# The first loads of a fused attention and MLP kernel in another order: two tiles of x, the q and k weights in two transfers, then the other two tiles

## The chip, the cores and the metric

The kernel runs on one core of one Trainium2 chip. The metric is device time in microseconds for one execution. A core has TensorE (PE, matmul), VectorE (DVE), ScalarE (ACT), GpSimd (POOL) and SyncE (SP, here an issuer of DMAs). Each runs its own instructions in order, and they wait for each other by semaphores. DMAs are issued by SP and ACT into a hardware queue each (q1 and q10 in the profile) and by GpSimd into a software queue.

## The reference

A pre-norm attention block with a dilated sliding window, then a pre-norm gated MLP (ReGLU), over 2048 rows of 512 in bf16:

```python
h  = x + A(layernorm(x))
h2 = h + B(layernorm(h))

def A(x):                         # 32 heads of 16, window of 8 keys, dilation 2
    q, k, v = split(x @ wqkv)     # wqkv: 512 x 1536
    logits[s, w] = q[s] . k[s - 2 w] * 16 ** -0.5      # w = 0..7, masked where s - 2 w < 0
    o[s] = sum_w softmax(logits[s])[w] * v[s - 2 w]
    return o @ wo                 # 512 x 512

def B(x):
    gate, up = x @ W_gate, x @ W_up                    # 512 x 1376 each
    return (relu(gate) * up) @ W_down                  # 1376 x 512
```

## The kernel before

The rows are worked in four chunks of 512 (`tk` = 0 to 3), each of four row tiles of 128 (`j` = 0 to 3). For a chunk the kernel normalises the rows, transposes them into `xnT`, projects to q, k and v, forms q*k products on VectorE, sums them per head with small matmuls, takes the softmax, multiplies by v on VectorE, applies `wo`, adds the residual, normalises again and runs the MLP. All steps of all chunks are put into one list by a planner (`Plan`): every step has an engine, a planned duration and dependencies, and a fixed table (`RANK`) gives each step its rank, so each engine's instructions stand in a fixed order. Load times enter the planner as constants (`xload`, `wload`), not from the DMA instructions themselves.

`setup()` runs ahead of the planned steps. It issues the first loads from SP and ACT alternately: `x_sm` tiles 0 to 3 (128 KB each, L291), `wqk_sb` in four transfers of 256 KB, one for each 128 rows of the q and k weights (L293), then from SP rows 512 to 1023 of x (512 KB, L294). GpSimd copies one element of tile 0 into `wv_sb` (L308) so that the load of the v weights (L309) goes out only after tile 0 has landed; the same trick at L310 holds the later chunks of x (L312) until rows 512 to 1023 have landed. Then come `wo`, the MLP weights, and constants built on GpSimd and VectorE. SP's later loads also wait for the completion of the transfer that used the same completion semaphore eight hardware DMAs earlier; in the profile that is L294, which waits for an x tile.

The first chunk's path, by line:

- L431 `bn_stats` and L434 `bn_aggr` on VectorE, for each row tile; L444 and L448 on ACT turn the variance into 1/std; L466 on VectorE normalises a tile into `row`.
- L495 transposes a tile on TensorE (four 128x128 matmuls), L511 (ACT, tiles 0 and 2) and L509 (VectorE, tiles 1 and 3) copy the transposed tile into `xnT` (`quad` in the profile).
- L385 is a run of 44 dummy matmuls on TensorE at the start, L393 eight more after the transposes of tile 0 and of tile 1.
- L536 is the projection. For the first four q and k outputs it is done in two halves: 256 columns (tiles 0 and 1), then the other 256 (tiles 2 and 3). On TensorE the order is: first halves of the first two outputs (8 matmuls), transposes of tiles 2 and 3, then 24 more half-width matmuls. The very first of them waits for all `wqk_sb` loads in turn and for the copy of tile 1.
- L544 copies the results out on ACT, and L583 forms the first q*k product on VectorE.

VectorE's order in the first chunk is: statistics of tiles 0 and 1, normalise tile 0, statistics of tile 3, normalise tile 1, statistics of tile 2, copy of transposed tile 1, normalise tiles 3 and 2, then statistics of the next chunk.

Of the kernel before, what the change touches and what calls it, by code (L numbers as in the profile page):

```python
# [190 lines left out]
def kernel(  # L191
# [11 lines left out]
    nc = tc.nc  # L203
    Bsz, S, D = A_x.shape
# [3 lines left out]
    NT = D // P  # L208
# [15 lines left out]
    BPC = CS // P  # L224
# [4 lines left out]
    x_rows = A_x.rearrange("b (tb p) d -> p (b tb) d", p=P)  # L229
# [20 lines left out]
    x_sm = sb.tile([P, NTB, D], BF16, name="x_sm")  # L250
    wqk_sb = sb.tile([P, NT, 2 * D], BF16, name="wqk_sb")
# [35 lines left out]
    def setup():  # L287

        w3_r = A_wqkv.rearrange("(dt p) f -> p dt f", p=P)
        for j in range(BPC):  # L290
            (nc.scalar if j % 2 else nc.sync).dma_start(x_sm[:, j:j + 1, :], x_rows[:, j:j + 1, :])  # L291
        for dt in range(NT):
            (nc.scalar if dt % 2 else nc.sync).dma_start(wqk_sb[:, dt:dt + 1, :], w3_r[:, dt:dt + 1, 0:2 * D])  # L293
        nc.sync.dma_start(x_sm[:, BPC:2 * BPC, :], x_rows[:, BPC:2 * BPC, :])  # L294
        nc.scalar.preload_act_table_set("natural_log_exp_and_others")
        V.memset(warm[:], 0.0)
        make_identity(nc, identity[:])
        nc.gpsimd.memset(eps_t[:], EPS)
        nc.gpsimd.iota(ci[:], pattern=[[0, 1]], base=0, channel_multiplier=1)
        nc.gpsimd.iota(sel_i[:], pattern=[[1, H]], base=0, channel_multiplier=0)  # L300
        nc.gpsimd.iota(sp_i[:], pattern=[[1, H], [0, DQ]], base=0, channel_multiplier=0)
        nc.gpsimd.iota(sm_i, pattern=[[0, 4], [1, H]], base=0, channel_multiplier=0)
        nc.gpsimd.iota(mk_i[:], pattern=[[1, PADL]], base=0, channel_multiplier=0)
        nc.gpsimd.memset(kT[:, :, 0:PADL], 0.0)
        nc.gpsimd.memset(vT[:, :, 0:PADL], 0.0)


        nc.gpsimd.tensor_copy(out=wv_sb[0:1, 0, 0:1], in_=x_sm[0:1, 0, 0:1])  # L308
        nc.sync.dma_start(wv_sb[:], w3_r[:, :, 2 * D:3 * D])  # L309
        nc.gpsimd.tensor_copy(out=x_sm[0:1, 2 * BPC, 0:1], in_=x_sm[0:1, BPC, 0:1])  # L310
        for tk in range(2, NCK):
            nc.sync.dma_start(x_sm[:, tk * BPC:(tk + 1) * BPC, :], x_rows[:, tk * BPC:(tk + 1) * BPC, :])  # L312

        nc.sync.dma_start(wo_sb[:], A_wo.rearrange("(p t) f -> p t f", t=NT))
        nc.sync.dma_start(wu_sb[:], B_W_up.rearrange("(dt p) f -> p dt f", p=P))
        nc.sync.dma_start(wg_sb[:], B_W_gate.rearrange("(dt p) f -> p dt f", p=P))
        nc.sync.dma_start(
            wd_sb[:, 0:NFF, :], B_W_down[0:NFF * P, :].rearrange("(ft p) n -> p ft n", p=P))
        if FTAIL:
            nc.sync.dma_start(wd_sb[:FTAIL, NFF, :], B_W_down[NFF * P:F, :])  # L320


        for n, (op, by) in enumerate(((ALU.arith_shift_right, 2), (ALU.bitwise_and, H - 1),
                                      (ALU.arith_shift_right, 5))):
            V.tensor_scalar(out=tmp[:, n:n + 1], in0=ci[:], scalar1=by, scalar2=None, op0=op)
        V.tensor_copy(out=cf[:, 0:3], in_=tmp[:])
        V.tensor_scalar(out=cf[:, 2:3], in0=cf[:, 2:3], scalar1=1.0 * DIL, scalar2=None, op0=ALU.mult)
        V.tensor_scalar(out=cf[:, 3:4], in0=cf[:, 2:3], scalar1=4.0 * DIL, scalar2=None, op0=ALU.add)
        V.tensor_scalar(out=sel[:], in0=sel_i[:], scalar1=cf[:, 0:1], scalar2=None, op0=ALU.is_equal)
        V.tensor_scalar(out=spread[:], in0=sp_i[:], scalar1=cf[:, 1:2], scalar2=None, op0=ALU.is_equal)  # L330
        V.tensor_scalar(out=same[:], in0=sm_i, scalar1=cf[:, 1:2], scalar2=None, op0=ALU.is_equal)
        for hf in range(2):
            V.tensor_scalar(out=mask[:, hf, :], in0=mk_i[:], scalar1=cf[:, 2 + hf:3 + hf],
                            scalar2=None, op0=ALU.is_ge)
# [540 lines left out]
    with tc.manual_schedule():  # L875
        setup()
        for op in todo:
            if op.fn is not None:
                op.fn()
# [35 lines left out]
```

## Time and profile before

| | before |
|---|---|
| runs, us | 201.94, 201.73, 202.31; median 201.94 |
| profiled execution, span from first to last instruction, us | 202.4 |
| TensorE busy | 194.1 us, 96% of the span |
| VectorE busy | 152.8 us, 75% |
| ACT busy | 111.1 us, 55% |
| granted TensorE clock, mean | 0.992 |
| x_sm loads of 128 KB, issue to landing | 2.8 us (SP) and 3.0 us (ACT), median |
| wqk_sb loads of 256 KB, issue to landing | 6.8 to 7.9 us, median 7.4 |
| x_sm rows 512 to 1023, issue to landing | 7.5 us |
| wv_sb load, issue to landing | 8.4 us |

The span runs from the first to the last instruction of one profiled execution; the profile states no other time for that execution, and the runs of the table are other executions. Times in the profile count from the span's start. An engine with a `q` behind its name is that engine's sequencer, which issues DMAs. "PEclk" is the granted TensorE clock, as a share of full speed. In a timeline a row gives start, length, engine, line, operation, what it writes and reads, how often, and in brackets how long the engine was idle before it and what ended that.

### The profile page before, as it was taken

The numbers are of one execution on the slowest core, as the hardware profiler recorded it, in microseconds if no ns is written. First come the engines' busy times: TensorE is split into PE (matmuls) and PEld (weight loads), VectorE is DVE, ScalarE is ACT, GpSimd is POOL, SyncE is SP. The second block draws the span as 40 slices with busy tenths as digits, with TensorE's granted clock in tenths as the row PEclk, the third lists the DMA queues.
The fourth block names the chain that finished last, engine by engine and source line by source line (L and its number), as shares of the span: only waits on it lengthen the run. The fifth ranks groups of instructions, "written<-read, shape, count | busy, mean of one in ns | idle before, by whom it ended". The sixth has DMA issues, their size and how long they took to land.

```text
span 202.4 us, 2934 instructions
## 1 busy us (share of the span) xinstructions
PE 194.1 (96%) x1072; PEld 97.0 (48%) x1091; DVE 152.8 (75%) x239; ACT 111.1 (55%) x232; POOL 12.7 (6%) x28
## 2 busy tenths in 40 slices
PE   8699999999999999998999999999999999999994
PEld 8585545555335444443444444444444444444542
DVE  6678999998999989998989768999966521142332
ACT  3337699766698855673641846802277821454700
POOL 3000000330000003300103100000000000000000
PEclk9969999999999999999999999999999999999999
DMA  5969980699000534996086883130200320002003
GB/s 147 322 201 328 409 265 19 135 189 177 3 0 0 130 80 78 191 181 172 3 156 129 163 211 100 26 79 0 78 29 0 74 56 0 0 3 78 0 0 130
DMA packets 21133, 21.97 MB, mean 109 GB/s; under 512 B 8736, under 2 KB 17920, under 8 KB 21120
## 3 DMA queue, kind: packets, MB, share of 16 engines
q1 hardware_dynamic: 18672, 14.65, 24.9%
q0 software_dynamic: 1728, 6.29, 16.9%
q10 hardware_dynamic: 720, 0.85, 1.2%
q8 instruction: 8, 0.13, 0.3%
q14 instruction: 5, 0.04, 0.1%
HBM read 8.42 MB, written 2.10 MB: 52 GB/s over the span
## 4 chain that ended last, share of the span: by engine, by line
PE 67%; DVE 12%; DMA 10%; issue 4%; ACT 4%; POOL 1%; SPq 1%; DVEq 0%; POOLq 0%; ACTq 0%
PE bank L800 29%; PE bank L845 18%; PE bank L536 11%; PE bank L762 5%; DVE big L710 5%; DVE big L583 4%; DMA big<-big 4%; DMA wqk_sb<-in_A_wqkv_dram 4%; PE bank L589 2%; DMA big<-ex 2%; ACT kT L544 2%; PE bank L495 1%; DVE row L466 1%; ACT quad L511 1%; POOL big L742 1%
## 5 line engine op out<-in xcount | busy, mean ns | idle before, releaser
L804 ACT CAST up_sb<-bank 128x512 bf16<-128x512 f32 (+1 forms) x44 | 25.0, 587 | 36.8 <-PE bank L800 33.3
L800 PE MATMUL bank<-quad,wu_sb 128*128 128x512 bf16 (+1 forms) x173 | 43.0, 379 | 0.7 <-ACT quad L511 0.4
L800 PE MATMUL bank<-quad,wg_sb 128*128 128x512 bf16 (+1 forms) x172 | 42.4, 379 | 0.1
L845 PE MATMUL bank<-wd_sb,gT 128*128 128x512 bf16 (+2 forms) x182 | 39.9, 366 | 0.4
L583 DVE TENSOR_TENSOR big<-quad,kT 128x4096 bf16<-128x4096 bf16 x16 | 36.2, 2288 | 1.6 <-ACT kT L544 0.7
L710 DVE TENSOR_TENSOR big<-big,vT 128x4096 bf16<-128x4096 bf16 x16 | 36.1, 2285 | 0.8 <-DMA big<-ex 0.8
L536 PE MATMUL bank<-quad,wqk_sb 128*128 128x512 bf16 (+1 forms) x140 | 31.4, 368 | 2.1 <-DMA wqk_sb<-in_A_wqkv_dram 1.9
L807 ACT ACTIVATE gr<-bank 128x512 bf16<-128x512 f32 (+1 forms) x44 | 25.7, 605 | 10.2 <-PE bank L800 5.4
L828 DVE TENSOR_TENSOR gT<-gr,up_sb 128x1024 bf16<-128x1024 bf16 (+1 forms) x24 | 15.2, 643 | 17.0 <-ACT gr L807 10.3
L845 PEld LDWEIGHTS <-gT 128*128 128x128 bf16 (+1 forms) x187 | 18.2, 98 | 20.1 <-DVE gT L828 0.6
L800 PEld LDWEIGHTS <-wu_sb 128*128 128x128 bf16 (+1 forms) x176 | 17.6, 100 | 21.0 <-DMA big<-ex 0.4
L800 PEld LDWEIGHTS <-wg_sb 128*128 128x128 bf16 (+1 forms) x176 | 17.4, 100 | 21.0 <-issue 1.3
L536 PEld LDWEIGHTS <-wqk_sb 128*128 128x128 bf16 x144 | 16.1, 117 | 14.5 <-DMA wqk_sb<-in_A_wqkv_dram 2.2
L856 DVE TENSOR_TENSOR row<-x_sm,bank 128x512 bf16<-128x512 bf16 (+1 forms) x17 | 10.6, 653 | 13.1 <-PE bank L845 13.1
L713 DVE TENSOR_TENSOR big<-big 128x1024 bf16<-128x1024 bf16 (+2 forms) x24 | 17.2, 733 | 1.7 <-DMA big<-big 1.6
L742 POOL DMA_DIRECT2D big<-big x12 | 10.5, 872 | 91.8 <-DVE big L710 48.5
L762 PE MATMUL bank<-wo_sb,quad 128*128 128x512 bf16 x63 | 15.4, 380 | 0.8 <-DVE quad L736 0.4
L536 PE MATMUL bank<-quad,wv_sb 128*128 128x512 bf16 x62 | 15.4, 380 | 0.1
L466 DVE TENSOR_SCALAR row<-x_sm,mv,rs 128x512 bf16<-128x512 bf16 x32 | 11.6, 407 | 3.2 <-ACT rs L448 3.2
L431 DVE BATCH_NORM_STATS2 st<-x_sm 128x6 f32<-128x512 bf16 x16 | 10.6, 672 | 3.2 <-DMA x_sm<-in_A_x_dram 3.2
L511 ACT COPY quad<-bank 128x1024 bf16<-128x1024 bf16 (+1 forms) x9 | 8.1, 921 | 8.5 <-PE bank L495 8.5
L544 ACT CAST kT<-bank 128x512 bf16<-128x512 f32 x16 | 9.1, 598 | 4.8 <-DVE big L583 3.5
(68 smaller groups left out, 140.3 us busy)
## 6 DMA issues: line engine op xcount, KB each, us to landing
big<-big POOLq DMA_DIRECT2D x12, 512.0 KB, 5.3
big<-ex SPq DMA_DIRECT2D x24, 128.0 KB, 3.1
out_dram<-row SPq DMA_DIRECT2D x15, 128.0 KB, 1.8
x_sm<-in_A_x_dram SPq DMA_DIRECT2D x3, 512.0 KB, 5.8
wu_sb<-in_B_W_up_dram SPq DMA_DIRECT2D x1, 1376.0 KB, 9.4
wg_sb<-in_B_W_gate_dram SPq DMA_DIRECT2D x1, 1376.0 KB, 12.5
wd_sb<-in_B_W_down_dram SPq DMA_DIRECT2D x1, 1280.0 KB, 15.5
wqk_sb<-in_A_wqkv_dram SPq DMA_DIRECT2D x2, 256.0 KB, 7.3
```

The costliest lines, as they stand in the source:

```text
L466: V.tensor_scalar(out=xn.t[:], in0=x, scalar1=mv.t[:, j, 0:1], scalar2=rs.t[:, j:j + 1], op0=ALU.add if residual else ALU.subtract, op1=AL ...
L536: nc.tensor.matmul(mm.t[:, lo:hi], lhsT=wv_sb[:, dt, t:D:NT] if c == 2 else wqk_sb[:, dt, c * D + t:(c + 1) * D:NT], rhs=xnT.t[:, dt, lo:h ...
L544: nc.scalar.copy(out=o, in_=mm.t[:])
L583: V.tensor_tensor(out=pb.t[:].rearrange("p (t w) s -> p t w s", t=2), in0=q4, in1=k4, op=ALU.mult)
L710: V.tensor_tensor(out=mt.t[:], in0=ab.t[:], in1=v8, op=ALU.mult)
L713: V.tensor_tensor(out=mt.t[:, 0:n, :], in0=mt.t[:, 0:n, :], in1=mt.t[:, n:2 * n, :], op=ALU.add)
L762: nc.tensor.matmul(od.t[:], lhsT=OT.t[:, t, j * P:(j + 1) * P], rhs=wo_sb[:, t, :], start=(t == 0), stop=(t == NT - 1 and tk not in RPE))
L800: nc.tensor.matmul(mm.t[:fs, lo:hi], lhsT=w_sb[:, dt, ft * P: ft * P + fs], rhs=hnT.t[:, dt, lo:hi], start=(dt == 0), stop=(dt == NT - 1))
L804: nc.scalar.copy(out=ub.t[:fs, i, :], in_=um.t[:fs, :])
L807: nc.scalar.activation(out=gr.t[:fs, i, :], in_=gm.t[:fs, :], func=ACT.Relu)
L828: V.tensor_tensor(out=gt.t[:fs, 0:n, :], in0=gr.t[:fs, 0:n, :], in1=ub.t[:fs, 0:n, :], op=ALU.mult)
L845: nc.tensor.matmul(od.t[:, c0:c1], lhsT=gts[ft].t[:fs, ft % 2, j * P:(j + 1) * P], rhs=wd_sb[:fs, ft, c0:c1], start=(ft == 0), stop=(ft == ...
```

## The change

The first eight loads become six in another order. SP and ACT each load one tile of x (rows 0 to 127 and 128 to 255), then each half of the q and k weights in one transfer of 512 KB (SP the first 256 weight rows, ACT the other 256), then each one more tile of x (rows 256 to 383 and 384 to 511). Rows 512 to 1023 follow from SP as before. No other instruction is changed, and the order on the compute engines stays the same; since two DMAs fewer go ahead, L294 no longer shares a completion semaphore with an earlier transfer and issues without a wait, and each first projection waits for two weight loads in place of four.

```diff
-        for j in range(BPC):
+        for j in range(2):
             (nc.scalar if j % 2 else nc.sync).dma_start(x_sm[:, j:j + 1, :], x_rows[:, j:j + 1, :])
-        for dt in range(NT):
-            (nc.scalar if dt % 2 else nc.sync).dma_start(wqk_sb[:, dt:dt + 1, :], w3_r[:, dt:dt + 1, 0:2 * D])
+        for q, dt in ((nc.sync, 0), (nc.scalar, 2)):
+            q.dma_start(wqk_sb[:, dt:dt + 2, :], w3_r[:, dt:dt + 2, 0:2 * D])
+        for j in range(2, BPC):
+            (nc.scalar if j % 2 else nc.sync).dma_start(x_sm[:, j:j + 1, :], x_rows[:, j:j + 1, :])
         nc.sync.dma_start(x_sm[:, BPC:2 * BPC, :], x_rows[:, BPC:2 * BPC, :])
```

Lines in the changed kernel stand two further down: L295 loads tiles 2 and 3, L296 rows 512 to 1023, and every later line has its number of before plus two.

## The prediction

> **What bounds the kernel now.** I read the chain of waits first, from the start of the span. It names the loads that the change touches.
>
> ```profile
> 1.67 0.42 SPq L293
> 2.09 0.04 issue
> 2.13 7.72 DMA wqk_sb<-in_A_wqkv_dram
> 9.85 0.05 issue
> 9.90 1.47 PE bank L536 x6
> 11.37 0.85 PE bank L495 x8
> 12.22 3.22 PE bank L536 x24
> ```
>
> The columns are start, length and what. The last of the four q, k weight transfers lands at 9.85 us, and from there to the end TensorE is nearly solid: from 16.73 to 31.00 us it is busy 14.22 of 14.27 us, and its waits after 16 us add up to about 1.3 us (0.4, 0.4, 0.3, 0.2). Whatever moves the first projection moves the end, close to one for one.
>
> Next the timeline of TensorE over the same stretch, for what it does while it waits.
>
> ```profile
> 0.99 4.87 PE L385 MATMUL bank<-warm 128*128 128x128 bf16 x44 [0.99 <-DVE warm L296]
> ...
> 6.96 0.61 PE L393 MATMUL bank<-warm 128*128 128x128 bf16 x8
> 8.54 0.47 PE L536 MATMUL bank<-quad,wqk_sb 128*128 128x256 bf16 x2 [0.98 <-DMA wqk_sb<-in_A_wqkv_dram]
> 9.90 1.47 PE L536 MATMUL bank<-quad,wqk_sb 128*128 128x256 bf16 x6 [0.88 <-DMA wqk_sb<-in_A_wqkv_dram]
> ```
>
> Two waits for weights, 0.98 and 0.88 us: 1.86 us is all that an earlier landing of the weights could return directly. The first projections use only rows 0 to 255 of x, so at first sight rows 256 to 511 can wait. The timeline of VectorE says otherwise:
>
> ```profile
> 5.09 0.38 DVE L466 TENSOR_SCALAR row<-x_sm,mv,rs 128x512 bf16<-128x512 bf16 x1
> 5.39 0.69 DVE L431 BATCH_NORM_STATS2 st<-x_sm 128x6 f32<-128x512 bf16 x1
> 5.99 0.40 DVE L466 TENSOR_SCALAR row<-x_sm,mv,rs 128x512 bf16<-128x512 bf16 x1
> 6.30 0.18 DVE L434 BATCH_NORM_AGGREGATE mv<-st 128x2 f32<-128x6 f32 x1
> 6.39 0.66 DVE L431 BATCH_NORM_STATS2 st<-x_sm 128x6 f32<-128x512 bf16 x1
> 7.09 0.18 DVE L434 BATCH_NORM_AGGREGATE mv<-st 128x2 f32<-128x6 f32 x1
> 7.19 0.39 DVE L509 COPY quad<-bank 128x512 bf16<-128x512 bf16 x1
> ```
>
> L431 at 5.39 is the statistics of row tile 3 (rows 384 to 511, loaded by ACT), and it stands ahead of L466 at 5.99, the normalisation of tile 1. L431 at 6.39 is tile 2's (loaded by SP), ahead of L509 at 7.19, which brings transposed tile 1 to SBUF. The first projection needs that copy (7.58). VectorE works through its list in order, and in the changed kernel the list is the same, entry for entry: RANK and the planner's load times are untouched. So tiles 2 and 3 are on the path of the first projection, through VectorE's queue.
>
> **The change, part by part.** *Weights earlier.* Each of the two hardware DMA queues (SP's q1 and ACT's q10, below called rings) carries 128 + 128 + 256 + 256 KB until the weights are in. Without x tiles 2 and 3 ahead, 256 KB fewer lie before them. Two stretches of the DMA view give the rate, first 2.9 to 3.5 us, then 4.5 to 6.5 us:
>
> ```profile
> DMA packets 243, 0.22 MB, mean 371 GB/s; under 512 B 28, under 2 KB 241, under 8 KB 243
> ```
>
> ```profile
> DMA packets 261, 0.49 MB, mean 245 GB/s; under 512 B 22, under 2 KB 22, under 8 KB 261
> ```
>
> 262 KB by 371 GB/s is 0.71 us, so the weights land at about 9.1 instead of 9.85 us. By itself this would be worth up to 0.7 us.
>
> *Tiles 2 and 3 later.* The second row also shows that a ring keeps its order: between 4.5 and 6.5 us only the 22 smallest packets (under 512 B, the completion writes) are under 2 KB; no 1 KB row of x gets past the 2 KB weight rows. Behind the weights, tiles 2 and 3 end where the weights end now, since each ring then has carried the same 768 KB: about 9.85 us instead of about 4.2 (issue at 1.21, landing 2.8 to 3.0 later). Bounds on that: had all 1.57 MB gone at 371 GB/s from the first packets at about 1.8, it would be 6.1 us; were the slow stretch (170 GB/s from 3.5 to 4.5 us, 186 from 4.5 to 5.5) twice as long, about 11.8. I take 9.85: the same bytes by the same engines, which run slowly on the first 2 KB rows in either order.
>
> *From that landing to the first projection.* By the VectorE rows, from the start of tile 3's statistics (5.39) to the end of tile 1's copy (7.58) is 2.19 us; tile 2 may land up to 1.0 later than tile 3 free of charge. On TensorE, tile 1's four transposes and eight fills follow the normalisation, which ends 1.0 after tile 3's statistics start. TensorE will have been idle since about 6.9 and run them slowly: 44 warm-up matmuls in 4.87 us are 111 ns each, 8 in 0.61 us are 76 with the tail, so 12 at some 107 ns from start to start are 1.3 us. That gives 2.3 to 2.4 after the landing: first projection at 9.9 + 2.3 = 12.2 us. Now it is in effect at 9.5 (six of the eight matmuls start at 9.90, the other two were done before). TensorE thus starts 2.7 us later, with the 0.7 us of the weights already inside.
>
> *The clock.* The windows of the span:
>
> ```profile
> core 0: us, PE busy (x) PEld busy (x) DVE busy (x) ACT busy (x) POOL busy (x), PEclk, DMA share, GB/s
> ...
> 6.49:9.91 3.42, 1.56 (x22) 1.14 (x19) 1.76 (x5) 1.28 (x5) 0.00 (x0) 1.00 0.98 341
> 9.91:13.32 3.41, 3.41 (x21) 2.67 (x22) 1.72 (x4) 0.59 (x1) 0.18 (x1) 0.50 0.45 152
> 13.32:16.73 3.41, 3.36 (x25) 2.74 (x25) 2.72 (x8) 2.06 (x4) 0.00 (x0) 1.00 0.83 261
> ```
>
> A stretch of 3.41 us in which TensorE was busy 1.56 us is followed by one at 0.50, and a full one by 1.00. So half speed is already paid for today, from 9.9 to 13.3, with TensorE full. A 256-column matmul takes 213 ns in it and 109 after it (24 of them between 12.01 and 15.28). In the changed kernel the projections from 12.2 on are 8 + 24 matmuls with 8 transposes between: 1.70 + 5.11 + 0.86 = 7.67 us at half speed, 3.9 at full.
>
> If the clock rose at 13.32 again, 1.12 us would pass slowly and the rest take (7.67 - 1.12) x 0.51 = 3.35, ending at 16.7 instead of 15.28: plus 1.4. If that stretch (TensorE busy from 10.95 on, 69% of it) does not count as busy, half speed lasts to 16.73: 16.73 + (7.67 - 4.53) x 0.51 = 18.3, plus 3.1. The rows bound the share that counts between 46% and nearly 100%. Taking 80%, and the grid of stretches at any place relative to the program, the clock rises between 13.7 and 17.1, on average 15.4: 15.4 + (7.67 - 3.2) x 0.51 = 17.7, plus 2.4.
>
> The Trainium skill (TensorE: Matmul & The Clock Gate, Part 1) states that full speed comes only after a sustained busy window of about 3.4 us, and that the window runs freely. By that, the clock rises between 14.4 and 17.8 on average at 16.1, and the sum would be plus 2.7 instead of 2.4; the 0.50 behind the half-idle stretch agrees.
>
> *What costs nothing.* ACT issues one DMA fewer, so its table load (2.64 to 3.92) comes some 0.45 us earlier; ACT's first use is at 4.48. The SP queue loses its wait of 1.1 us ahead of L294 (rows 512 to 1023), which goes out at about 2.1 instead of 3.66, but stays behind the weights and tile 2 in its ring: still about 11.2, and wanted only after the normalisation of tiles 2 and 3, then ending at 12.9. GpSimd's copy at L308 waits for tile 0 alone, so L309 (v weights) issues as now and lands near 12.5, needed after 18. The statistics of rows 512 to 1023 (three of them from 12.60 to 15.67) slip with the copy ahead of them, to about 18.6; the first product L583 can then start at 16.3 + 2.4 = 18.7. If the clock is kind they are 0.2 us late.
>
> The sum is plus 2.4 us. The profiled execution's span is 202.4 us, the median 201.94; I put the sum on each: 204.8 for an execution like the profiled one, 204.3 for the median.
>
> **Rivals.** *Tiles 2 and 3 land early (faster).* The slow stretch vanishes with two requests of 512 KB. At 6.1 us the first projection could begin at 8.4, TensorE would hardly idle, the clock would stay up, and 8.4 + 3.9 = 12.3 against 15.28 is minus 3, about 199. Break-even is a landing at about 7.4: projection at 9.8, half speed from 9.9 to 13.3, end at 15.4. For it: from 9.0 on the rings run at 380 GB/s, so the slowness is no fixed rate. Against it: it sits where the first weight rows are fetched, and they are fetched in both orders. The Trainium skill (DMA: Bandwidth & Descriptors, Bandwidth) has a rule to this side, larger transfers come nearer the peak; no run here shows it yet. 8 in 100 for faster, 6 for a landing near break-even.
>
> *The slow stretch shrinks in part.* Landing at 8.0 to 9.2: projection at 10.4 to 11.5, plus 0.6 to 1.8: 202.5 to 203.7. 18 in 100.
>
> *It grows.* Both rings now begin the weights at once and may stall one another: landing at 11.0 to 11.8, plus 3.6 to 4.4: 205.5 to 206.3. 10 in 100.
>
> *The order is not what the lists show.* If VectorE could take tile 1's normalisation first, only 0.7 us of earlier weights would count: 201.2. The list leaves this no room; it is inside the 8.
>
> **How the numbers follow.** The forecast, landing within half a us of 9.85 and a clock anywhere between the two ends, has 58 in 100 and spans 203.0 to 205.4. With the neighbours on both sides the range is 202.3 to 205.9; outside it lie the faster case and the worst of the last. A measurement of this kernel tells about 0.3%, 0.6 us (the three runs span 201.73 to 202.31). Faster 0.08, within 0.06, slower 0.86.
>
> **What would show it.** Right: VectorE idle ahead of the third or fourth L431, released by DMA x_sm at 9 to 10.5 us; TensorE idle from about 7 to 11; the first L536 at about 12.2, released by DVE L509 and not by a weight DMA; half clock past 13.3. Wrong: the third L431 starting before 7.4, or the first L536 still waiting for wqk_sb; or a first projection later by 2.7 us with the end not later, which would mean that slack after 16 us took it up.

## The result, and the profile after

| | before | changed |
|---|---|---|
| median of 5 runs each, us | 201.74 (201.31 to 202.31) | 204.69 (202.87 to 205.24) |
| ratio to before | 1 | 1.0121, 95% interval 1.0085 to 1.0157 |
| the same kernel again (8 runs, beside 25 of before), us | 201.92 | 203.40; ratio 1.0073, interval 1.0046 to 1.0099 |
| span of the profiled executions, us | 202.4, and 199.7 in a second profile | 201.6, and 201.7 in a second profile |

The change makes the kernel slower by about 1%: 204.3 us was forecast. Most executions take 1.7 to 1.8 us more than their span (201.6 us of span for 203.33 us). Read that against the profile of before: its span of 202.4 would be an execution of 204.1 us, above every one of the five in the table. That execution was unusual, and a second profile of the unchanged kernel (the first experiment below) is the one to compare with.

The chain of waits of the changed kernel starts thus (start, length, what):

```profile
1.66 5.53 DMA x_sm<-in_A_x_dram
7.19 0.02 issue
7.22 0.04 DVE st L433
7.25 0.57 issue
7.83 0.40 DVE row L468
...
9.56 1.87 PE bank L538 x8
11.43 0.85 PE bank L497 x8
12.29 2.65 PE bank L538 x24
```

The transfer on the chain is now that of x, no longer that of the weights, and what follows it is VectorE's work on tiles 3 and 2. The timeline of VectorE in the changed kernel shows the stall where it was expected:

```profile
5.10 0.38 DVE L468 TENSOR_SCALAR row<-x_sm,mv,rs 128x512 bf16<-128x512 bf16 x1
7.22 0.69 DVE L433 BATCH_NORM_STATS2 st<-x_sm 128x6 f32<-128x512 bf16 x1 [1.74 <-DMA x_sm<-in_A_x_dram]
7.83 0.40 DVE L468 TENSOR_SCALAR row<-x_sm,mv,rs 128x512 bf16<-128x512 bf16 x1
...
9.02 0.39 DVE L511 COPY quad<-bank 128x512 bf16<-128x512 bf16 x1
```

L433 at 7.22 is tile 3's statistics; VectorE stood idle for 1.74 us for it, with tile 1's normalisation (7.83) waiting behind. TensorE, in its own timeline:

```profile
5.77 0.61 PE L395 MATMUL bank<-warm 128*128 128x128 bf16 x8
8.28 0.40 PE L497 MATMUL bank<-identity,row 128*128 128x128 bf16 x4 [1.90 <-DVE row L468]
8.52 0.78 PE L395 MATMUL bank<-warm 128*128 128x128 bf16 x8
9.56 1.87 PE L538 MATMUL bank<-quad,wqk_sb 128*128 128x256 bf16 x8 [0.27 <-ACT rs L446]
```

In the last row the profile names ACT (L446) as what ended the wait, because that ended last. The copy of tile 1 ended at 9.41 us (9.02 + 0.39), 0.15 us before the projection, and with VectorE's list altered (below) the row names the copy, with the same 0.15 us between (6.94 and 7.09), so I read the copy as the releaser here too.

No wait for weights is left; 1.90 us of waiting for VectorE has come instead, in one piece. The first projection starts at 9.56 us. What that piece does to the clock stands in the windows of this kernel, cut where its clock changes:

```profile
5.39:8.80 3.41, 1.51 (x27) 1.33 (x25) 1.68 (x5) 1.33 (x5) 0.01 (x1) 1.00 1.08 366
8.80:12.22 3.42, 3.15 (x23) 2.39 (x21) 1.89 (x6) 0.90 (x4) 0.16 (x1) 0.50 0.80 268
12.22:15.63 3.41, 3.36 (x28) 2.97 (x28) 3.24 (x9) 2.23 (x5) 0.00 (x0) 1.00 0.95 311
```

TensorE is busy 1.51 of 3.41 us while it waits, and the next 3.42 us run at half clock, over the first eight projections.

One thing is unlike the forecast. The DMA view of the changed kernel from 3.5 to 4.5 and from 4.5 to 6.5 us:

```profile
DMA packets 182, 0.37 MB, mean 371 GB/s; under 512 B 1, under 2 KB 1, under 8 KB 182
...
DMA packets 566, 0.77 MB, mean 387 GB/s; under 512 B 51, under 2 KB 325, under 8 KB 566
```

Before, these stretches moved 170 and 245 GB/s. The slow stretch is gone, the weights are in at 6.60 us, and tiles 3 and 2 land at 7.19 and 7.40.

### The profile page after: what moved, and what is told of

The parts are those of the page before. It is cut to its first block, busy times and chain, and to the rows that moved or that the text cites. A ratio compares the mean times of both kernels' runs of the same rounds, so it can differ in the third digit from the quotient of the medians.

```text
span 201.6 us, 2931 instructions
## 1 busy us (share of the span) xinstructions
PE 193.1 (96%) x1072; PEld 96.5 (48%) x1091; DVE 152.8 (76%) x239; ACT 111.2 (55%) x232; POOL 12.7 (6%) x28
## 4 chain that ended last, share of the span: by engine, by line
PE 67%; DVE 12%; DMA 9%; issue 5%; ACT 4%; POOL 1%; ACTq 0%; DVEq 0%; POOLq 0%
PE bank L802 29%; PE bank L847 18%; PE bank L538 11%; PE bank L764 5%; DVE big L712 5%; DVE big L585 5%; DMA big<-big 4%; DMA x_sm<-in_A_x_dram 3%; PE bank L591 2%; DMA big<-ex 2%; ACT kT L546 2%; PE bank L497 1%; DVE row L468 1%; ACT quad L513 1%; POOL big L744 1%
## 5 line engine op out<-in xcount | busy, mean ns | idle before, releaser
L585 DVE TENSOR_TENSOR big<-quad,kT 128x4096 bf16<-128x4096 bf16 x16 | 36.2, 2285 | 1.0 <-ACT kT L546 0.8
L538 PE MATMUL bank<-quad,wqk_sb 128*128 128x512 bf16 (+1 forms) x140 | 30.7, 364 | 0.5 <-ACT rs L446 0.3
L433 DVE BATCH_NORM_STATS2 st<-x_sm 128x6 f32<-128x512 bf16 x16 | 10.6, 672 | 2.0 <-DMA x_sm<-in_A_x_dram 2.0
```

Source lines behind the costliest of these rows:

```text
L538: nc.tensor.matmul(mm.t[:, lo:hi], lhsT=wv_sb[:, dt, t:D:NT] if c == 2 else wqk_sb[:, dt, c * D + t:(c + 1) * D:NT], rhs=xnT.t[:, dt, lo:h ...
L585: V.tensor_tensor(out=pb.t[:].rearrange("p (t w) s -> p t w s", t=2), in0=q4, in1=k4, op=ALU.mult)
```

## The experiments

Each ratio is to runs of before made beside the experiment, 23 to 29 of them, with a 95% interval behind it.

**Before again, for a second profile.** No edit.

> The kernel before, unchanged, for a second profile of it. In the first profile of before the last q, k weights landed at 9.85 us and the span was 202.4 us; in the profile of the changed kernel they landed at 6.6 us and the span was 201.6 us, though its median is 2.95 us above that of before. If the late landing is the usual one: weights again at 9.5 to 10 us, span 202 us or more. If it was an outlier of that one execution: weights at 6.5 to 8 us, no stretch at half clock after the first projection, span near 200 us. Either way a time of 201.3 to 202.3 us.

Measured: 201.88 us, ratio 1.0014 (0.9992 to 1.0036). Its timeline of TensorE:

```profile
7.80 0.39 PE L536 MATMUL bank<-quad,wqk_sb 128*128 128x256 bf16 x2 [0.44 <-ACT rs L444]
8.98 0.94 PE L536 MATMUL bank<-quad,wqk_sb 128*128 128x256 bf16 x6 [0.79 <-DMA wqk_sb<-in_A_wqkv_dram]
9.76 0.61 PE L495 MATMUL bank<-identity,row 128*128 128x128 bf16 x8
```

and its windows around the first projection:

```profile
4.98:8.39 3.41, 2.61 (x35) 1.92 (x32) 3.31 (x11) 2.14 (x8) 0.00 (x0) 1.00 0.93 296
8.39:11.80 3.41, 2.54 (x25) 2.19 (x26) 1.36 (x3) 0.58 (x1) 0.18 (x1) 1.00 0.71 237
```

The span is 199.7 us. The weights land in two steps with matmuls between (the last on SP's queue at 8.94), so TensorE's waits are short (0.44 and 0.79), every window is busy for 2.5 us or more, and the clock stays up. The weights still land late, within 1 us of the first profile; what was unusual there is the half clock. Of 89 executions of before in which the clock was recorded, 3 have a mean granted clock below 0.995 (203.81 to 204.09 us); the others have a median of 201.84. The guess in the expectation that the weights themselves would land at 6.5 to 8 us was wrong.

**The transfers alone.** All four x tiles first as before, then two weight transfers.

```diff
-        for dt in range(NT):
-            (nc.scalar if dt % 2 else nc.sync).dma_start(wqk_sb[:, dt:dt + 1, :], w3_r[:, dt:dt + 1, 0:2 * D])
+        for q, dt in ((nc.sync, 0), (nc.scalar, 2)):
+            q.dma_start(wqk_sb[:, dt:dt + 2, :], w3_r[:, dt:dt + 2, 0:2 * D])
```

> Only the shape is changed: all four x tiles first, as before, then the q, k weights in two transfers of 512 KB. Queue theory (the loss comes from tiles 3 and 2 landing late, because VectorE takes their statistics ahead of tile 1): as before, within 0.6 us. Transfer theory (the loss comes from fewer, larger requests): slower by 2 to 3 us, as the full change.

Measured: 202.54 us, ratio 1.0059 (1.0033 to 1.0084), so a real part: neither theory. It is 0.9 us over before, less than the 2.95 us of the changed kernel's first five runs, but its interval overlaps that of the next eight (1.0046 to 1.0099). The first projection can't start on half the weights any more, as its timeline shows:

```profile
9.37 1.07 PE L536 MATMUL bank<-quad,wqk_sb 128*128 128x256 bf16 x8 [2.00 <-DMA wqk_sb<-in_A_wqkv_dram]
```

One wait of 2.00 us stands in place of two short ones. That isn't all of it. VectorE's list also holds the statistics of a tile of the third chunk of x ahead of the first product (L583), and here they wait for their load, in this kernel first and then in the second profile of before:

```profile
15.49 0.69 DVE L431 BATCH_NORM_STATS2 st<-x_sm 128x6 f32<-128x512 bf16 x1 [1.26 <-DMA x_sm<-in_A_x_dram]
```

```profile
14.12 0.69 DVE L431 BATCH_NORM_STATS2 st<-x_sm 128x6 f32<-128x512 bf16 x1 [0.25 <-DMA x_sm<-in_A_x_dram]
```

The product starts at 16.11 for 14.73 us, and the eight projections behind the next chunk's transposes at 20.42 for 19.53. TensorE had finished the work before those transposes at about 19.00 us, where the second profile of before is at 18.63. At that point, then, some 0.4 of the 0.9 us comes from the weights and the rest from VectorE, in one profile each. This profile has no half clock, but 3 of 12 executions show it (203.81 to 204.17 us); the other nine have a median of 202.16.

**The order alone.** Tiles 0 and 1, four weight transfers of 256 KB, tiles 2 and 3.

```diff
-        for q, dt in ((nc.sync, 0), (nc.scalar, 2)):
-            q.dma_start(wqk_sb[:, dt:dt + 2, :], w3_r[:, dt:dt + 2, 0:2 * D])
+        for dt in range(NT):
+            (nc.scalar if dt % 2 else nc.sync).dma_start(wqk_sb[:, dt:dt + 1, :], w3_r[:, dt:dt + 1, 0:2 * D])
```

(against the changed kernel)

> Only the order is changed: x tiles 0 and 1, then the q, k weights in four transfers of 256 KB, then x tiles 2 and 3. Queue theory: all of the loss, plus 2 to 3.5 us over before, and VectorE idle ahead of the third statistics until that tile lands behind the weights. Transfer theory: as before, within 0.6 us.

Measured: 205.00 us, ratio 1.0163 (1.0126 to 1.0199). The order suffices for the whole loss. In its profile VectorE waits 3.60 us for tile 3, until 8.85, the first projection starts at 11.19, and half clock lasts 6.83 us: a granted clock of 0.982, as in 4 of 6 executions (0.981 to 0.983).

**VectorE's order.** In the changed kernel, tile 1 is normalised and copied out ahead of the statistics of tiles 3 and 2.

```diff
                 queues[op.eng].append(op)
+            dve = queues["DVE"]
+            keys = ("xxn1", "xtv1", "xst3", "xag3", "xst2", "xag2", "xxn3", "xxn2")
+            own = {o.key[0]: o for o in dve if o.key and o.key[1] == 0 and o.key[0] in keys}
+            at = sorted((i for i, o in enumerate(dve) if o in own.values()), reverse=True)
+            for i, k in zip(at, keys, strict=True):
+                dve[i] = own[k]
```

> The changed kernel with VectorE's order altered in the first chunk alone: tile 1 is normalised and its transpose copied out before the statistics of tiles 3 and 2. Queue theory: the first projection no longer waits for tiles 3 and 2 and starts with the weights, at 7.3 to 7.8 us where they land by 7; at least half of the loss comes back: plus 0 to 1.5 us over before, the rest being the second halves, which still wait for tiles 3 and 2. If VectorE's queue were not the cause: as the changed kernel, plus 2.5 to 3.5 us.

Measured: 202.53 us, ratio 1.0047 (1.0018 to 1.0076). The timeline of TensorE in this kernel:

```profile
7.09 1.04 PE L544 MATMUL bank<-quad,wqk_sb 128*128 128x256 bf16 x8 [0.16 <-DVE quad L517]
10.14 0.70 PE L503 MATMUL bank<-identity,row 128*128 128x128 bf16 x8 [2.01 <-DVE row L474]
```

The first projection starts 2.5 us earlier than in the changed kernel (7.09 for 9.56), with the same loads: VectorE's queue held it. Of the loss 0.87 us is left, where the changed kernel's two comparisons have 2.95 and 1.48 us. Against the second the intervals overlap, so how much of the time returns is not settled; that the projection moves is. The second halves need tiles 2 and 3 all the same, and the wait (2.01 us) has moved behind the first eight matmuls; 5 of 12 executions show the half clock (203.44 to 204.18 us), the other seven have a median of 202.16.

**The clock, taken out.** In the changed kernel, 28 dummy matmuls for 8 behind tile 0's transposes.

```diff
-                        fill(ds[-1])
+                        fill(ds[-1], 28 if j == 0 else NFILL)
```

(`fill` takes the number as an argument.)

> The changed kernel with 28 dummy matmuls in place of 8 behind the transposes of tile 0, so that TensorE is busy until about 7.5 us (8.9 if it is still at half clock) while it waits for tiles 3 and 2; nothing else. If the half clock after that wait is part of the loss: fewer executions with a granted clock of 0.992 or less, and 0.5 to 1.7 us of the 2.95 come back, the rest being the wait itself. If the clock has no part: as the changed kernel, plus 2.5 to 3.5 us over before.

Measured: 202.57 us, ratio 1.0026 (1.0011 to 1.0040), and a granted clock of 0.999 or 1.000 in all 12 executions. Nothing is faster in the loads or on VectorE. The chain of waits in this kernel, and then in the second profile of the changed kernel, where tile 3 landed at 7.47 (7.49 here):

```profile
9.86 1.04 PE bank L538 x8
10.90 0.45 PE bank L497 x8
11.34 2.62 PE bank L538 x24
...
19.14 0.89 PE bank L497 x16
```

```profile
12.54 2.62 PE bank L538 x24
15.16 0.05 issue
15.21 5.13 PE bank L538 x23
20.34 0.89 PE bank L497 x16
```

The projection begins at 9.86 in the one and 9.84 in the other; the transposes of the next chunk (x16) follow at 19.14 and at 20.34. The half clock alone is 1.20 us. The same point stands at 18.63 in the second profile of before: the wait alone, with whatever the 20 more dummies cost, is 19.14 - 18.63 = 0.51 us. The medians, of runs made side by side, go the same way: 201.92 for before, 202.57 with the dummies, 203.40 for the changed kernel.

**Tiles 2 and 3 by GpSimd.** Taken out of the queues of SP and ACT.

```diff
-        for j in range(2, BPC):
-            (nc.scalar if j % 2 else nc.sync).dma_start(x_sm[:, j:j + 1, :], x_rows[:, j:j + 1, :])
...
         nc.gpsimd.memset(vT[:, :, 0:PADL], 0.0)
+        for j in range(2, BPC):
+            nc.gpsimd.dma_start(x_sm[:, j:j + 1, :], x_rows[:, j:j + 1, :])
```

> The changed kernel with x tiles 2 and 3 issued by GpSimd into its own software queue, after its constants, and no longer behind the weights in the queues of SP and ACT. Queue theory (they are late because of their place in those queues): they land at 4.5 to 6.5 us, the first projection is bound by the weights again, and the time is that of before or up to 0.7 us less, because the weights have 256 KB less ahead of them. If any order with the weights earlier costs the time: still plus 2 us or more.

Measured: 205.74 us, ratio 1.0184 (1.0151 to 1.0217): the expectation failed. Issued at 2.39 and 3.10, they land at 8.54 and 9.00; the DMA view of 5 to 6 us has no packet of the software queue, that of 6 to 7 has the first 24. So the test of the place in the queue was spoilt by another delay. It still says what a late tile costs: statistics at 9.03, projection at 11.37.

**Tiles 2 and 3 between the weights.** The edit is shown against the changed kernel.

```diff
-        for q, dt in ((nc.sync, 0), (nc.scalar, 2)):
-            q.dma_start(wqk_sb[:, dt:dt + 2, :], w3_r[:, dt:dt + 2, 0:2 * D])
+        for dt in (0, 1):
+            (nc.scalar if dt % 2 else nc.sync).dma_start(wqk_sb[:, dt:dt + 1, :], w3_r[:, dt:dt + 1, 0:2 * D])
         for j in range(2, BPC):
             (nc.scalar if j % 2 else nc.sync).dma_start(x_sm[:, j:j + 1, :], x_rows[:, j:j + 1, :])
+        for dt in (2, 3):
+            (nc.scalar if dt % 2 else nc.sync).dma_start(wqk_sb[:, dt:dt + 1, :], w3_r[:, dt:dt + 1, 0:2 * D])
```

> x tiles 0 and 1, then the first two q, k weight transfers of 256 KB, then x tiles 2 and 3, then the other two weight transfers. By the working of the prediction tiles 2 and 3 then land at 5 to 7 us, before the point (about 7.4) from which their landing decides, and the last weights land as in before: within 0.6 us of before, perhaps up to 1 us over it in executions where the first weights are slow. If weights ahead of any x tile cost the time in themselves: plus 1.5 us or more.

Measured: 201.60 us, ratio 0.9994 (0.9960 to 1.0029). Tiles 3 and 2 land at 6.00 and 6.30, the first projection starts at 8.37, and the clock falls in 1 of 12 executions. Its rows of tile 3's statistics and of the first projection:

```profile
6.02 0.69 DVE L435 BATCH_NORM_STATS2 st<-x_sm 128x6 f32<-128x512 bf16 x1 [0.45 <-DMA x_sm<-in_A_x_dram]
...
8.37 1.04 PE L540 MATMUL bank<-quad,wqk_sb 128*128 128x256 bf16 x8 [0.44 <-ACT rs L448]
```

Against the order alone, with the same 256 KB transfers, tiles 2 and 3 go one transfer further ahead in each queue, and the loss is gone: this, not the one by GpSimd, is the test of the place in the queue.

**The changed kernel again.** No edit.

> The changed kernel once more, for more executions and a second profile: 203 to 205.5 us. Queue theory: VectorE idle ahead of the third statistics until tile 3 lands, at 7 to 10 us. Clock theory: most executions with a granted clock of 0.992 or less, where before has 0.998 to 1.000 in most; executions with one more stretch at half clock (0.008 of the mean clock) are longer by 1 to 1.7 us.

Measured: 203.40 us, ratio 1.0073 (1.0046 to 1.0099). With the first five, 10 of 13 executions have a granted clock of 0.992 or less (median 203.71 us), 3 have 1.000 (202.09 to 202.94). The first comparison, of five runs each, stood high; 1.0% is what both intervals allow.

**The clock, put in.** The kernel before without the 16 dummy matmuls behind tiles 0 and 1.

```diff
-    NWARM, NFILL = 44, 8
+    NWARM, NFILL = 44, 0
```

> The kernel before without the 16 dummy matmuls behind the transposes of tiles 0 and 1, so that TensorE idles longer while it waits for the weights; the loads are as before. This asks for the clock's part by itself, in the old load order. Clock theory: stretches of 3.41 us with TensorE busy under about half come up here too, the mean granted clock falls to 0.992 in half or more of the executions (before: 1 in about 60), and the median rises by 1 to 2 us with no load moved. If the clock is only a by-product: same as before, within 0.6 us.

Measured: 201.60 us, ratio 0.9990 (0.9964 to 1.0016). The half clock comes as expected, in 7 of 12 executions, and these are longer (median 202.39) than the other five (201.07) by 1.3 us. The median of all did not rise, against the expectation: without the dummies the executions at full clock came out about 0.8 us below those of before. Why is not settled.

**An attempt at a faster version.** Tiles between the weights, and two moves in VectorE's list: tile 1's normalisation ahead of tile 3's statistics, the copy of tile 3 (`xtv3`) ahead of the next chunk's first statistics.

```diff
+            keys = ("xxn1", "xst3", "xag3", "xtv1", "xst2", "xag2", "xxn3", "xxn2")
...
+            i = next(i for i, o in enumerate(dve) if o.key == ("xtv3", 0))
...
+            dve[i], dve[i + 1] = dve[i + 1], dve[i]
```

> An attempt at a faster version: the loads of the run with tiles 2 and 3 between the two weight pairs, and VectorE's order changed at two places: tile 1 normalised ahead of tile 3's statistics, and the copy of transposed tile 3 ahead of the next chunk's first statistics. By the profile of the run without the second change the first projection (8.37 us) then starts with the last weights, at about 7.8, and the second halves some 0.3 us earlier: 0.3 to 0.6 us below that run, 201.0 to 201.4 us, a gain of 0.2% to 0.4% over before. If the second halves are bound by tiles 2 and 3 alone: no gain.

Measured: 201.95 us, ratio 1.0014 (0.9993 to 1.0036): no gain. In its profile tile 3 landed at 7.10, not 6.00, and the second halves waited for it as the second expectation said. No version tried here beats before.

## Why the prediction was right or wrong

**VectorE's order: right, and shown.** The forecast put tiles 3 and 2 on the path of the first projection, 2.3 us from the start of tile 3's statistics to the projection. Measured where they bound it:

| run | tile 3's statistics | first projection | between |
|---|---|---|---|
| tiles between the weights | 6.02 | 8.37 | 2.35 |
| changed | 7.22 | 9.56 | 2.34 |
| changed, again | 7.49 | 9.84 | 2.35 |
| order alone | 8.85 | 11.19 | 2.34 |
| by GpSimd | 9.03 | 11.37 | 2.34 |

Altering VectorE's list alone moved the projection to 7.09. Of the signs that the forecast named, three came about: VectorE idles ahead of the third statistics, TensorE idles behind VectorE, and the first projection no longer waits for weights. Their times did not: tile 3's statistics start at 7.22 and 7.49, on both sides of the 7.4 that was to show it wrong, the first projection at 9.56 and 9.84 in place of 12.2, and half clock ends at 12.22 and 12.39, not past 13.3.

**The landing at 9.85: wrong by 2.4 to 2.7 us.** It was 7.2 to 7.5, which is the rival "near break-even" that had 6 in 100. The failed step is "the same bytes by the same engines, which run slowly on the first 2 KB rows in either order". The slow stretch does not come with every order: from 4 to 7 us the four profiles with four x tiles first (before, before again, transfers alone, no dummies) move 244, 226, 253 and 308 GB/s; the five with both 512 KB weight transfers behind two tiles move 384 to 396; 256 KB transfers behind two tiles move 281, 326 and 355. The rule on larger transfers that the forecast quoted from the Trainium skill (DMA: Bandwidth & Descriptors, Bandwidth) is borne out by the last two groups, but not by the transfers alone (253). In these profiles neither the order nor the size by itself gives 384 GB/s or more; the two together do. Why the old order is slow was not tried.

So the weights came in at 6.60, earlier by far more than the 0.7 us of the sum. It bought nothing, because the projection waited for x.

**"So half speed is already paid for today": wrong.** That was true of the one profile at hand and of 3 in 89 executions. The changed kernel brings the half clock in 10 of 13. This is the larger part of the loss: by the rows above, 1.20 us of 1.71, the wait itself 0.51; by the medians 0.83 of 1.48.

**The sum: right by two errors.** The plus 2.4 us was worked out against the first profile of before. Against that execution the changed one is shorter (201.6 for 202.4), as the forecast's own break-even at a landing of about 7.4 says. It was then added to the median of 201.94, which belongs to executions of about 200 us of span without the half clock. So the base was 2.7 us too long (202.4 for 199.7) and the landing 2.5 us too late, and the two cancel. Worked again from the second profiles: 199.7 + 0.5 + 1.2 is 201.4, and 201.7 was measured. The forecast's range of 203.0 to 205.4 for a landing within half a us of 9.85 held the median without its reason, by luck.

**"Close to one for one": right for a delay, not for a gain.** The eight projections behind the next chunk's transposes start at 19.53 us in the second profile of before, 20.04 with 28 dummies, 21.01 and 21.23 in the changed kernel; the spans are 199.7, 200.4, 201.6 and 201.7. With the tiles between the weights they start at 18.91, earlier by 0.62, and the span is 199.8: the gain is lost later. Where was not followed, and each is one profile.

**The share that counts as busy: right as far as it goes.** In these profiles the clock falls behind windows with TensorE busy 1.0 to 1.6 us of 3.41, and not behind 1.88 (the transfers alone, 5.42 to 8.83 us), 2.04 (the attempt at a faster version, 6.61 to 10.02) or more. It rises again behind 2.9 to 3.4 us and not behind 1.5 or 2.1, as the windows of the kernel with GpSimd's loads show:

```profile
8.77:12.18 3.41, 2.09 (x16) 1.80 (x17) 3.12 (x9) 1.00 (x4) 0.18 (x1) 0.50 0.75 243
12.18:15.60 3.42, 3.42 (x22) 2.67 (x20) 1.77 (x5) 0.59 (x1) 0.00 (x0) 0.50 0.95 338
```

The assumed 80% lies within the bounds for the rise. It isn't the share for the fall: 1.88 us of work (55%) kept the full clock, 2.09 us (61%) at half clock did not bring it back. The 0.50 that the forecast set beside the rule on full speed is a fall, and that rule is about the rise. The Trainium skill (TensorE: Matmul & The Clock Gate, Part 1) has the clock fall after at least one idle window; here a window with up to 1.6 us of work in it is enough, and the measurement decides.

**Costs put at nothing:** the statistics of rows 512 to 1023 and the table load showed no new wait: L585 in the changed kernel starts at 15.82 with no idle time ahead of it, where before it had waited 0.66 us for ACT.

## What to carry to other kernels

Before a load is put back, look for the first instruction that waits for it on every in-order queue, and at what stands behind it there: the data may not be needed yet, and the queue may be. Look at a wait's length against the clock as well: the 1.90 us in one piece cost more by the half clock after it (1.2 us) than by the wait (0.5). And see whether the one profile at hand is an ordinary execution, by setting its span against the runs; here two wrong terms gave the right number.

## What the runs showed of the hardware

- TensorE's clock falls with no idle window at all: a gap of 1.9 to 2.1 us sufficed when it left 1.3 to 1.5 us of work in 3.41. A gap of 2.00 us that left 1.88 us of work in the window did not lower it, and filling the changed kernel's gap with 20 more dummy matmuls kept the clock at 0.999 or 1.000 in 12 of 12 executions.
- The rate at which the first loads move, from 4 to 7 us, depends on their order and size: 226 to 308 GB/s with four tiles of x ahead of the weights, 281 to 355 with two ahead and weights in 256 KB transfers, 384 to 396 with two ahead and 512 KB transfers.
- The first DMAs issued by GpSimd, at 2.39 and 3.10 us, moved no packet before 6 us, beside two busy hardware queues, in one profile.
